# A DFT mixer and a 16-head attention on one core: the two middle rows of the sequence matrix prepared once, new durations in the planner, a second buffer for the spread maxima

## The chip, the core and the metric

The kernel runs on one core of one Trainium2 chip. A core has five engines that run side by side, each through its own list of instructions in order: TensorE (PE, matrix products, with its weight loads shown as PEld), VectorE (DVE), ScalarE (ACT), GpSimd (POOL) and SyncE (SP), which here issues every transfer. The metric is device time in microseconds of one launch. Before the change it was 798.91 us, the median of three runs (797.62 to 800.2).

## The reference

Two independent halves write the left and the right 448 columns of one output of 2048 rows.

```python
# A: Fourier mixing, real part
a = einsum("bsd,ed->bse", x, dft_hid_re);  b = einsum("bsd,ed->bse", x, dft_hid_im)
y = einsum("ts,bse->bte", dft_seq_re, a) - einsum("ts,bse->bte", dft_seq_im, b)
# B: attention, 16 heads of 28
q, k, v = split_heads(x @ wqkv)
o = softmax(q @ k.T * 28 ** -0.5) @ v
return concatenate([y, o @ wo], axis=-1)
```

`x` is 2048 x 448 in both, the sequence matrices `dft_seq_re` and `dft_seq_im` are 2048 x 2048, all in float32. Products are made in two parts, a rounded high part and the rest as a low part, so that the fast matrix format keeps enough digits.

## The kernel before

**The attention.** Part B projects `x` to queries, keys and values and keeps them in device memory. For each of 16 heads it computes scores in tiles of 128 keys by 512 queries (line 1155), takes the exponential from PSUM to a buffer called `kept` on ScalarE (line 1161), and multiplies with the values (line 1138). There are 16 buffers (pairs) called `kept`, and many steps borrow them. For the first tile of keys of each head, `first_tiles` takes the largest score per query and spreads it: VectorE turns the scores in blocks (line 1101) into a buffer `mb`, reduces them (line 1102), gathers (1108 to 1113), and for four chunks of queries turns the maxima back into `mb` (line 1122). From there they go to one row of `q` (line 1125, VectorE or GpSimd) and are added to the scores (line 1127, VectorE or GpSimd) ahead of the exponential (line 1129). There is one `mb`, so a second chunk can't be turned until line 1127 of the first has read it. The scores of the other key tiles need the row written by line 1125.

**The Fourier half.** The sequence matrices are symmetric about their middle, so the kernel works with 8 folded tiles of 128 inputs and 8 of 128 outputs. `hidden` makes the hidden transform of the folded `x`, for the real part and then for the imaginary part (line 900), and adds up `acc` for output row 1024 (line 921; from it comes the small product at line 1253). `sequence` then multiplies by the sequence matrix: for each of 8 output tiles and each half `g` (0 or 1) it loads four blocks of 256 KB: `w` (line 580), and the three others at line 638, two of them from a turned copy `wr` of the matrix. `w` is rounded on GpSimd (line 458) and its low part taken (line 591). `mirrored` compares the four blocks with each other: differences (lines 654, 672; "either" engine), single columns (lines 659, 662; "small"), and largest absolute values (line 645, VectorE), which decide at the end whether the matrices have the symmetry that the fast path takes for granted. If they had not, a slow general path would run. The blocks live in 8 buffers called `wraw`, and a buffer can take the next load only after line 645 has read it.

The first row and row 1024 have no partner, and enter by one more matmul for each output tile: three rows of the summed row `ext` against `peaks`, the hidden transform of the inputs 0 and 1024. In the kernel before, `mirrored` makes `ext` for each tile when `g` is 0, out of row 0 of the sum of line 672, by four VectorE instructions on 1 x 128 elements: line 677 rounds it, line 678 copies it, line 679 takes the low part, line 681 clears the row in the block. That is done 16 times.

**What sets the order.** Nothing is reordered by hand or by the chip. Each step is handed to a planner (`Schedule`) with a key (when it is wanted), the engines that may do it, a duration for each engine, and the buffers it takes. The planner plays all engines forward by these durations: an engine that is free takes the ready step with the smallest key, and the step is emitted there. So durations in the code change nothing about an instruction, but they decide which of VectorE and GpSimd gets a step, and in which order the five engines and the transfers run. On the chip each engine then waits, in that order, for what is not done.

The table of these durations is spread over the code: `either = {"POOL": 1.25, "DVE": 0.69}` and `small = {"POOL": 0.2, "DVE": 0.15}` for `mirrored`, 0.35 us for line 921, 0.8 us on VectorE for line 1127, 0.15 and 0.12 for `ext`.

Of the kernel before, what the change touches and what calls it, by code (L numbers as in the profile page):

```python
# [11 lines left out]
F32 = mybir.dt.float32  # L12
# [338 lines left out]
def tile_kernel(ctx, tc, xa, wre, wim, wd, xb, wqkv, wo, out):  # L351
# [33 lines left out]
    x_raw, x_hl = new("xraw", [P, NH, 4], F32), new("xhl", [P, 2, NH, 4], F32R)  # L385
    ext_s, peaks = new("ext", [P, P], F32R, 2), new("peak", [P, 2, E], F32R)
    w_hi, w_lo = new("whi", [P, 3, 4, P], F32R), new("wlo", [P, 3, 4, P], F32R)
# [5 lines left out]
    kept_s = new("kept", [P, 2, CH], F32, NKEPT)  # L393
    mb_s = new("mb", [P, CH], F32, 1, True)
    sm_s = new("sm", [P, 2, NT], F32, 2)
# [47 lines left out]
    def dve(key, emit, d=DVE_P, **kw):  # L443
        return sch.add({"DVE": d}, key, lambda e: emit(), **kw)
# [129 lines left out]
    class Piece:  # L574


        def __init__(self, src, key, kind="c", early=False, home=None, after=(), wide=False):
            self.hi, self.lo = whi.slot(), wlo.slot()
            raw = self.raw = home or wraw.slot()
            ld = self.ld = dma(key, lambda: nc.sync.dma_start(raw.t, src()), deps=after, acq=[raw])  # L580
            if kind == "c":
                a = sch.add({"POOL": 1.0, "ACT": ACT_S} if wide else {"POOL": 1.0}, key + 1, lambda g: eng_copy(g, self.hi.t, raw.t),
                            deps=[ld], acq=[self.hi], use=[raw])
            else:
                a = act(key + (0 if early else 1), lambda: nc.scalar.activation(self.hi.t, raw.t, AF.Copy), ACT_S, soon=SOON,  # L585
                        deps=[ld], acq=[self.hi], use=[raw])
            at = key + (0 if early else 1.5)
            both = ("DVE",) if early else ("POOL", "DVE") if wide else ("POOL",)
            e = {g: {"DVE": 0.8, "POOL": 1.25}[g] for g in both}
            n = 4 if kind == "c" else 3  # L590
            b = sch.add(e, at, lambda g: eng[g].tensor_tensor(  # L591
                self.lo.t[:, :n], raw.t[:, :n], f32(self.hi.t)[:, :n], op=ALU.subtract),
                deps=[a], acq=[self.lo], use=[raw, self.hi])
            self.ready, self.hi_ready, self.lo_ready = [b], a, [b]
            if kind == "w":
                self.ready.append(sch.add({g: {"DVE": 0.3, "POOL": 0.53}[g] for g in both}, at, lambda g: eng[g].tensor_tensor(
                    self.lo.t[:64, 3], raw.t[:64, 3], f32(self.hi.t)[:64, 3], op=ALU.subtract),
                    deps=[a, b], use=[raw, self.hi, self.lo]))
# [48 lines left out]

    either = {"POOL": 1.25, "DVE": 0.69}
    small = {"POOL": 0.2, "DVE": 0.15}

    def mirrored(part, tt, g, w, w2, w3, w4, left, right, key):
# [22 lines left out]
        if g == 0:  # L674
            ext = ext_s.slot()
            row = lambda: w2.raw.t[:1, 3, :]
            c = dve(key, lambda: nc.vector.tensor_copy(ext.t[:1], row()), 0.15, deps=[a, *ext_clear], acq=[ext], use=[w2.raw])
            c = dve(key, lambda: nc.vector.tensor_copy(ext.t[32:33], f32(ext.t)[:1]), 0.12, deps=[c], use=[ext])
            c = dve(key, lambda: nc.vector.tensor_tensor(ext.t[64:65], row(), f32(ext.t)[:1], op=ALU.subtract), 0.12,
                    deps=[c], use=[ext, w2.raw])  # L680
            a = dve(key, lambda: nc.vector.memset(row(), 0.0), 0.1, deps=[c], use=[w2.raw])
        else:
            ext, c = None, None
        largest(lambda: w2.raw.t, [a], part, key + 1, [w2.raw])
        return ext, c

    edge_done, edge_free = {}, {}
    far_done = []
# [146 lines left out]
    ext_clear += [pool(41.0, lambda: nc.gpsimd.memset(f32(peaks), 0.0), 0.57)]  # L835
    for i, t in enumerate(ext_s.tiles):
        ext_clear.append(pool(42.0 + i, lambda t=t: nc.gpsimd.memset(f32(t), 0.0), 0.3))
    ld = [dma(112.0 + 3 * k, lambda k=k: nc.sync.dma_start(x_raw[:, :, k], xa[NH:, :, k, 0].rearrange("t p -> p t")), 64, 2.0) for k in range(4)]
# [21 lines left out]
    class Pair:  # L860


        def __init__(self, i, part, key):
# [12 lines left out]
            c = sch.add({"DVE": 0.3, "POOL": 0.53}, key + 1.5, lambda g: eng[g].tensor_tensor(  # L876
                self.hi.t[64:, 3:], raw.t[64:, 3:], f32(self.hi.t)[64:, 3:], op=ALU.subtract), deps=[a], use=[raw, self.hi])
            self.ready = [b, c]

    def hidden(part, weights, ready, after):  # L880
# [25 lines left out]
        for i in range(NH):  # L906
# [10 lines left out]
                    deps=[t], use=[o, ut])  # L917
            a = act(key - 10, lambda ut=ut, uh=uh: nc.scalar.activation(uh, ut.t, AF.Copy), 0.3, soon=SOON, deps=[t, *after], use=[ut])
            b = sch.add({"POOL": 0.62, "DVE": 0.35}, key - 10, lambda e, ut=ut, uh=uh, ul=ul: eng[e].tensor_tensor(
                ul, ut.t, f32(uh), op=ALU.subtract), deps=[a], use=[ut])  # L920
            acc_done.append(dve(key - 5, lambda ut=ut, i=i: nc.vector.scalar_tensor_tensor(
                acc[:, part], ut.t, mid[:, part, i:i + 1], acc[:, part], op0=ALU.mult, op1=ALU.add), 0.35,
                deps=[t, got, acc_done[-1]], use=[ut]))
            if i == 0:
# [25 lines left out]
    def sequence(part, made, tiles=range(NH), late=False, free=()):  # L950
        src, wr = wim if part else wre, wr_d[part]
        u = u_of[part]
        for tt in tiles:
            o, pair = fill_s.slot(), kept_s.slot()
            for g in range(2):
# [13 lines left out]
                x, x_ready = mirrored(part, tt, g, w, w2, w3, w4, left, right, key - 8)  # L969
                if g == 0:  # L970
                    ext, ext_ready = x, x_ready
                jobs = []
                for k in range(4):
                    i = 4 * g + k
                    pair2 = [(w.hi, k, u[:, i, :], [w.hi_ready], w.hi, i), (w.lo, k, u[:, i, :E], w.ready, w.lo, i)]
                    if g and k == 3:
                        jobs.append((ext, None, peaks[:65, part], [ext_ready, *done_top[part]], ext, 0))
                        pair2.reverse()
                    jobs += pair2
                for n, (slot, k, b, ready, use, i) in enumerate(jobs):  # L980
                    first, final = g == 0 and n == 0, g == 1 and n == 8

                    def emit(e, o=o, slot=slot, k=k, b=b, first=first, final=final):
                        a = slot.t[:65] if k is None else slot.t[:, k, :]
                        nc.tensor.matmul(o.t[:, :2 * E if slot.pool is whi else E], a, b, start=first, stop=final)  # L985
                    deps = [last[0], *ready]
                    if tt == 0:
                        deps += made[i]
                    last[0] = pe(key + n * M225, emit, d=M448 if slot.pool is whi else M225, deps=deps, acq=[o] if first else [],
                                 use=[use, *([] if first else [o])])  # L990
                    if first:
# [3 lines left out]
                if part == 0:  # L995
                    if tt == 0 and g == 0:
                        turn_edges(1, last[0], key)
                    for n in range(2):
                        turn_rows(1, (tt * 2 + g) * 2 + n, last[0], key)
            key = key - 60  # L1000
            if part == 0:
# [4 lines left out]
            else:  # L1006
# [4 lines left out]
                b = dve(key, lambda o=o, q=q: nc.vector.tensor_tensor(q(), o.t[:, E:2 * E], q(), op=ALU.add), 0.35, deps=[b], use=[o, py])  # L1011
                w2 = {"DVE": 0.35, "POOL": 0.62}
                parts = {}
# [70 lines left out]
    def first_tiles(h):  # L1084
# [34 lines left out]
        for c in range(NC):  # L1119
# [6 lines left out]
                               deps=[t], use=[mb, q]))  # L1126
            sh = sch.add({"DVE": 0.8, "POOL": POOL_2}, key, lambda e, s=s, mb=mb: eng[e].tensor_tensor(s.t, s.t, mb.t, op=ALU.add),  # L1127
                         deps=[t, made[c]], use=[s.pair, mb], lat=LAT_S)
# [356 lines left out]
```

## Time and profile before

| what | value |
|---|---|
| median of three runs | 798.91 us (797.62 to 800.2) |
| the profiled execution, its time | 797.84 us |
| its span, first to last instruction | 796.2 us |
| mean granted TensorE clock | 0.973 |
| PE busy | 757.2 us (95%) |
| ACT busy | 610.7 us (77%) |
| DVE busy | 533.2 us (67%) |
| POOL busy | 336.5 us (42%) |
| DMA, share of 16 engines | 55.1% |

Busy time of PE counts matmuls whose ends are modelled, so a busy PE need not be at its peak. A granted clock under 1 means that the chip let TensorE run at less than full speed for part of the time. "Idle before, releaser" in a row of groups tells what an engine waited for just ahead of those instructions. The chain of waits starts at the last instruction and goes back, at each step, to what released it.

### The profile page before, as it was taken

What the parts mean: (1) busy time and instruction counts of PE and PEld (TensorE: products, weight loads), DVE (VectorE), ACT (ScalarE), POOL (GpSimd) and SP (SyncE); (2) the same over time, 40 slices, a digit from 0 to 9 for tenths busy, and PEclk for the clock granted to TensorE, in tenths of its full rate; (3) what the DMA queues carried; (4) which work ended last, traced back from release to release, by engine and by line L of the source; (5) the groups of instructions that cost most, each with busy time, mean ns of one, the idle gap of its engine ahead of it and who ended that gap; (6) DMA issues with size and microseconds to landing.
All of it is one profiled execution on the core that took longest, in us unless ns stands there. A gap on an engine that the chain in (4) does not pass through costs nothing.

```text
span 796.2 us, 13074 instructions
## 1 busy us (share of the span) xinstructions
PE 757.2 (95%) x4150; PEld 428.5 (54%) x4150; DVE 533.2 (67%) x1039; ACT 610.7 (77%) x1232; POOL 336.5 (42%) x410
## 2 busy tenths in 40 slices
PE   9999999999999998988899999998988799999997
PEld 7898655555555553454345554444444344334496
DVE  5547814465466869898887967796967878244371
ACT  6403798989898988887688979896876768898932
POOL 7301301414032535566573716274767754022510
PEclk9999999999999999999799999999998999999999
DMA  8957836472428456726477666646556462305254
GB/s 307 289 207 219 250 115 182 150 224 85 130 63 231 145 160 179 222 71 198 131 222 189 195 172 194 182 129 198 176 171 210 154 191 74 88 19 171 80 172 145
DMA packets 113541, 133.15 MB, mean 167 GB/s; under 512 B 50314, under 2 KB 63145, under 8 KB 113465
## 3 DMA queue, kind: packets, MB, share of 16 engines
q1 hardware_dynamic: 113464, 132.24, 55.1%
q8 instruction: 35, 0.57, 0.3%
q14 instruction: 42, 0.34, 0.1%
HBM read 101.15 MB, written 49.19 MB: 189 GB/s over the span
## 4 chain that ended last, share of the span: by engine, by line
PE 68%; DVE 18%; DMA 6%; ACT 4%; issue 2%; SPq 0%; POOL 0%; DVEq 0%; ACTq 0%
PE bank L1155 22%; PE bank L1138 21%; PE bank L726 12%; PE bank L1317 4%; DMA wraw<-wr 4%; ACT kept L1161 3%; PE bank L985 3%; DVE far L645 2%; PE bank L762 2%; PE bank L900 2%; PE bank L1096 1%; DVE mb L1101 1%; DVE qm L1102 1%; DVE kept L1127 1%; DVE q L1125 1%
## 5 line engine op out<-in xcount | busy, mean ns | idle before, releaser
L1161 ACT ACTIVATE kept<-bank 128x512 f32<-128x512 f32 x960 | 485.8, 646 | 83.7 <-PE bank L1155 82.6
L1155 PE MATMUL bank<-q,k 98*128 98x512 f32 x960 | 343.4, 430 | 17.7 <-ACT kept L1161 11.7
L1155 PEld LDWEIGHTS bank<-q,k 98*128 98x128 f32 x960 | 174.5, 190 | 191.1 <-issue 99.2
L1138 PE MATMUL bank<-kept,v 128*32 128x512 f32 x2048 | 251.4, 615 | 0.0
L1138 PEld LDWEIGHTS bank<-kept,v 128*32 128x32 f32 x2048 | 55.8, 111 | 121.1 <-issue 116.3
L1127 POOL TENSOR_TENSOR kept<-kept,mb 128x512 f32<-128x512 f32 x39 | 55.5, 1423 | 70.0 <-DVE mb L1122 52.2
L1100 ACT ACTIVATE kept<-bank 128x512 f32<-128x512 f32 x64 | 38.4, 653 | 35.2 <-PE bank L1096 22.6
L1101 DVE STREAM_TRANSPOSE mb<-bank 128x512 f32<-128x512 f32 x64 | 45.5, 711 | 26.9 <-PE bank L1096 23.6
L1198 POOL TENSOR_TENSOR kept<-kept 128x512 f32<-128x512 f32 x16 | 20.6, 1288 | 96.3 <-DVE kept L1193 78.6
L645 DVE TENSOR_REDUCE far<-wraw 128x1 f32<-128x508 f32 (+1 forms) x90 | 57.5, 657 | 1.1 <-POOL wraw L672 0.7
L726 PE MATMUL bank<-big,whi 128*128 128x512 f32 x154 | 56.6, 396 | 0.0
L1122 DVE STREAM_TRANSPOSE mb<-am 128x512 f32<-128x512 f32 x64 | 45.1, 705 | 11.8 <-POOL kept L1127 10.3
L591 POOL TENSOR_TENSOR wlo<-wraw,whi 128x512 fp32r<-128x512 f32 (+1 forms) x34 | 45.0, 1324 | 18.8 <-ACT whi L585 16.8
L985 PE MATMUL bank<-big,whi 128*128 128x452 f32 x128 | 49.8, 390 | 3.1 <-POOL whi L458 3.1
L1129 ACT ACTIVATE kept<-kept 128x512 f32<-128x512 f32 x64 | 43.0, 704 | 10.1 <-POOL kept L1127 5.6
L654 POOL TENSOR_TENSOR wraw<-wraw,wraw 128x508 f32<-128x508 f32 x35 | 38.6, 1104 | 23.6 <-DMA wraw<-wr 19.6
L1102 DVE TENSOR_REDUCE qm<-mb 128x16 f32<-128x512 f32 x64 | 43.4, 678 | 1.2
L1125 POOL CAST q<-mb 1x512 fp32r<-1x512 f32 x20 | 13.5, 673 | 71.5 <-DVE mb L1122 55.3
L726 PE MATMUL bank<-wd,big 128*128 128x448 f32 x176 | 36.8, 364 | 0.0
L985 PE MATMUL bank<-big,wlo 128*128 128x226 f32 x128 | 35.8, 279 | 0.9 <-POOL wlo L591 0.9
L1189 DVE STREAM_TRANSPOSE kept<-kept 128x512 f32<-128x512 f32 x16 | 11.2, 702 | 35.5 <-ACT kept L1187 35.5
L726 PE MATMUL bank<-big,wlo 128*128 128x512 f32 x88 | 34.8, 396 | 0.0
(167 smaller groups left out, 966.3 us busy)
## 6 DMA issues: line engine op xcount, KB each, us to landing
wraw<-wr SPq DMA_DIRECT2D x60, 256.0 KB
qkd<-kept SPq DMA_DIRECT2D x40, 256.0 KB
wraw<-xa SPq DMA_DIRECT2D x32, 256.0 KB
wraw<-wre SPq DMA_DIRECT2D x32, 256.0 KB
wr<-wre SPq DMA_DIRECT2D x31, 256.0 KB
wr<-wim SPq DMA_DIRECT2D x31, 256.0 KB
k<-qkd SPq DMA_DIRECT2D x64, 112.0 KB
q<-qkd SPq DMA_DIRECT2D x64, 112.0 KB
```

What stands on the lines that cost most here:

```text
L591: b = sch.add(e, at, lambda g: eng[g].tensor_tensor(self.lo.t[:, :n], raw.t[:, :n], f32(self.hi.t)[:, :n], op=ALU.subtract), deps=[a], acq ...
L645: far_done.append(dve(key, lambda: nc.vector.tensor_reduce(far[:, part, n:n + 1], t(), axis=AX.XY, op=ALU.max, apply_absolute_value=True), ...
L726: nc.tensor.matmul(o.t[:, :cols], w(), x(), start=(i == 0), stop=(i == n - 1))
L985: nc.tensor.matmul(o.t[:, :2 * E if slot.pool is whi else E], a, b, start=first, stop=final)
L1101: t = dve(key, lambda o=o, tm=tm: nc.vector.transpose(tm.t, o.t), 0.73, deps=[m], acq=[tm], use=[o], lock=[o], own=RAW_S)
L1102: rs.append(dve(key, lambda tm=tm, c=c: nc.vector.tensor_reduce(qm.t[:, 0, c * NT:(c + 1) * NT], tm.t.rearrange("p (j r) -> p j r", r=32), ...
L1122: t = dve(key, lambda mb=mb, c=c: nc.vector.transpose(mb.t, f32(am.t)[:, c * NT:(c + 1) * NT].unsqueeze(2).to_broadcast([P, NT, 32])), 0.7 ...
L1127: sh = sch.add({"DVE": 0.8, "POOL": POOL_2}, key, lambda e, s=s, mb=mb: eng[e].tensor_tensor(s.t, s.t, mb.t, op=ALU.add), deps=[t, made[c] ...
L1129: shown.append(act(key, lambda s=s: nc.scalar.activation(s.t, s.t, AF.Exp, scale=SCALE), ACT_S, deps=[sh], use=[s.pair]))
L1138: nc.tensor.matmul(o.t[c * VW:(c + 1) * VW, :], VT[h].t[:, kt // 4, kt % 4, :], tiles[c].t, start=(kt == 0), stop=(kt == NT - 1))
L1155: m = pe(key, lambda e, o=o, q=q, kt=kt: nc.tensor.matmul(o.t, KT[h][kt // 4].t[:KM, kt % 4 * P:(kt % 4 + 1) * P], q.t[:KM, :], start=True ...
L1161: es[h, kt].append(act(key - 20, lambda o=o, p=p: nc.scalar.activation(p.t, o.t, AF.Exp, scale=SCALE), deps=[m], use=[o, p.pair]))
```

## The change

Four edits, of which the third and the fourth are spread over several places.

1. `ext` is no longer made for each output tile. A new function `middle(part, ...)` loads rows 0 and 1024 of the matrix, 8 x 128 elements each, onto one partition (two transfers of 4 KB into two `kept` buffers), combines them, and writes the three rows for all eight tiles at once, 1 x 1024 elements, into a part of `big` that is free by then. It is called for the real part behind the fifth tile of `hidden(0)` and for the imaginary part at the seventh output tile of the real part. The four steps may run on GpSimd or VectorE; one GpSimd memset goes ahead of them. The matmul takes its 128 columns out of that strip. Only the clearing of the row in the block (line 681) stays in `mirrored`. The two `ext` buffers and their two memsets go.
2. `mb` gets a second buffer.
3. Durations that the planner reckons with are set to other values, most of them higher on VectorE, some lower on GpSimd.
4. The matmul's step in `sequence` no longer takes an `ext` buffer.

```diff
-    ext_s, peaks = new("ext", [P, P], F32R, 2), new("peak", [P, 2, E], F32R)
+    peaks = new("peak", [P, 2, E], F32R)
-    mb_s = new("mb", [P, CH], F32, 1, True)
+    mb_s = new("mb", [P, CH], F32, 2, True)
...
-                a = sch.add({"POOL": 1.0, "ACT": ACT_S} if wide else {"POOL": 1.0}, key + 1, lambda g: eng_copy(g, self.hi.t, raw.t),
+                a = sch.add({"POOL": 0.75, "ACT": ACT_S} if wide else {"POOL": 0.75}, key + 1, lambda g: eng_copy(g, self.hi.t, raw.t),
-            e = {g: {"DVE": 0.8, "POOL": 1.25}[g] for g in both}
+            e = {g: {"DVE": 0.85, "POOL": 1.35}[g] for g in both}
...
-    either = {"POOL": 1.25, "DVE": 0.69}
-    small = {"POOL": 0.2, "DVE": 0.15}
+    either = {"POOL": 1.2, "DVE": 0.83}
+    small = {"POOL": 0.35, "DVE": 0.4}
...
         if g == 0:
-            ext = ext_s.slot()
-            row = lambda: w2.raw.t[:1, 3, :]
-            c = dve(key, lambda: nc.vector.tensor_copy(ext.t[:1], row()), 0.15, deps=[a, *ext_clear], acq=[ext], use=[w2.raw])
-            c = dve(key, lambda: nc.vector.tensor_copy(ext.t[32:33], f32(ext.t)[:1]), 0.12, deps=[c], use=[ext])
-            c = dve(key, lambda: nc.vector.tensor_tensor(ext.t[64:65], row(), f32(ext.t)[:1], op=ALU.subtract), 0.12,
-                    deps=[c], use=[ext, w2.raw])
-            a = dve(key, lambda: nc.vector.memset(row(), 0.0), 0.1, deps=[c], use=[w2.raw])
-        else:
-            ext, c = None, None
+            a = dve(key, lambda: nc.vector.memset(w2.raw.t[:1, 3, :], 0.0), 0.17, deps=[a], use=[w2.raw])
...
+    def middle(part, key, dep):
+        src, pairs = (wre, wim)[part], [kept_s.slot() for _ in range(2)]
+        h = NH * P
+        op = ALU.add if part else ALU.subtract
+        ext = big[:, 2 * NT * E + part * h:2 * NT * E + (part + 1) * h]
+        row = lambda i: pairs[i].t.rearrange("p a b -> p (a b)")[:1, :h]
+        z = pool(key, lambda: nc.gpsimd.memset(f32(ext)[:65], 0.0), 1.1, deps=[dep])
+        ld = [dma(key + 0.1 * i, lambda i=i: nc.sync.dma_start(
+            row(i).rearrange("p (a b) -> p a b", a=NH), src[:NH, :1, NH * i, :].rearrange("t p s -> p t s")), 8, 2.0,
+            deps=[dep], acq=[pairs[i]]) for i in range(2)]
+        both = {"POOL": 1.5, "DVE": 1.3}
+        a = sch.add(both, key + 1, lambda g: eng[g].tensor_tensor(row(1), row(1), row(0), op=op), deps=ld, use=pairs)
+        b = sch.add(both, key + 1, lambda g: eng[g].tensor_copy(ext[:1], row(1)), deps=[a, z], use=[pairs[1]])
+        c = sch.add(both, key + 1, lambda g: eng[g].tensor_copy(ext[32:33], f32(ext)[:1]), deps=[b])
+        d = sch.add(both, key + 1, lambda g: eng[g].tensor_tensor(ext[64:65], row(1), f32(ext)[:1], op=ALU.subtract),
+                    deps=[b], use=[pairs[1]])
+        middles[part] = ext, [c, d]
...
-    for i, t in enumerate(ext_s.tiles):
-        ext_clear.append(pool(42.0 + i, lambda t=t: nc.gpsimd.memset(f32(t), 0.0), 0.3))
...
-            a = pool(key + 1, lambda: nc.gpsimd.tensor_copy(self.hi.t, raw.t), 1.0, deps=[b], acq=[self.hi], use=[raw])
-            b = sch.add(either, key + 1.5, lambda g: eng[g].tensor_tensor(
+            a = pool(key + 1, lambda: nc.gpsimd.tensor_copy(self.hi.t, raw.t), 0.7, deps=[b], acq=[self.hi], use=[raw])
+            b = sch.add({"POOL": 1.08, "DVE": 0.58}, key + 1.5, lambda g: eng[g].tensor_tensor(
...
-                acc[:, part], ut.t, mid[:, part, i:i + 1], acc[:, part], op0=ALU.mult, op1=ALU.add), 0.35,
+                acc[:, part], ut.t, mid[:, part, i:i + 1], acc[:, part], op0=ALU.mult, op1=ALU.add), 0.7,
...
+            if part == 0 and i == 4:
+                middle(0, key, a)
...
-                        jobs.append((ext, None, peaks[:65, part], [ext_ready, *done_top[part]], ext, 0))
+                        jobs.append((None, None, peaks[:65, part], [*ext_ready, *done_top[part]], None, 0))
...
-                        a = slot.t[:65] if k is None else slot.t[:, k, :]
+                        a = ext[:65, tt * P:(tt + 1) * P] if k is None else slot.t[:, k, :]
...
+            if part == 0 and tt == NH - 2:
+                middle(1, key, last[0])
...
-                w2 = {"DVE": 0.35, "POOL": 0.62}
+                w2 = {"DVE": 0.64, "POOL": 0.7}
...
-            sh = sch.add({"DVE": 0.8, "POOL": POOL_2}, key, lambda e, s=s, mb=mb: eng[e].tensor_tensor(s.t, s.t, mb.t, op=ALU.add),
+            sh = sch.add({"DVE": 0.92, "POOL": POOL_2}, key, lambda e, s=s, mb=mb: eng[e].tensor_tensor(s.t, s.t, mb.t, op=ALU.add),
```

Left out of the diff: line 918 is planned at 0.45 us for 0.3, line 919 at 0.77 (GpSimd) or 0.64 (VectorE) for 0.62 or 0.35, and line 876 at 0.5 on VectorE for 0.3.

More of the change, by code (lines that the diff above doesn't have):

```diff
@@ L674, in mirrored @@
         if g == 0:
-            ext = ext_s.slot()
-            row = lambda: w2.raw.t[:1, 3, :]
-            c = dve(key, lambda: nc.vector.tensor_copy(ext.t[:1], row()), 0.15, deps=[a, *ext_clear], acq=[ext], use=[w2.raw])
-            c = dve(key, lambda: nc.vector.tensor_copy(ext.t[32:33], f32(ext.t)[:1]), 0.12, deps=[c], use=[ext])
-            c = dve(key, lambda: nc.vector.tensor_tensor(ext.t[64:65], row(), f32(ext.t)[:1], op=ALU.subtract), 0.12,
-                    deps=[c], use=[ext, w2.raw])
-            a = dve(key, lambda: nc.vector.memset(row(), 0.0), 0.1, deps=[c], use=[w2.raw])
-        else:
-            ext, c = None, None
-        largest(lambda: w2.raw.t, [a], part, key + 1, [w2.raw])
-        return ext, c
+            a = dve(key, lambda: nc.vector.memset(w2.raw.t[:1, 3, :], 0.0), 0.17, deps=[a], use=[w2.raw])
+        largest(lambda: w2.raw.t, [a], part, key + 1, [w2.raw])
+    def middle(part, key, dep):
[15 more added lines that the diff above has]
+        middles[part] = ext, [c, d]
+    middles = {}
     edge_done, edge_free = {}, {}
@@ L872, in __init__ @@
                 raw.t[:, :, 0], x_raw[:, back], raw.t[:, :, 0], op=op), deps=[a, *x_col], use=[raw])
-            a = pool(key + 1, lambda: nc.gpsimd.tensor_copy(self.hi.t, raw.t), 1.0, deps=[b], acq=[self.hi], use=[raw])
-            b = sch.add(either, key + 1.5, lambda g: eng[g].tensor_tensor(
+            a = pool(key + 1, lambda: nc.gpsimd.tensor_copy(self.hi.t, raw.t), 0.7, deps=[b], acq=[self.hi], use=[raw])
+            b = sch.add({"POOL": 1.08, "DVE": 0.58}, key + 1.5, lambda g: eng[g].tensor_tensor(
                 self.lo.t[:, :3], raw.t[:, :3], f32(self.hi.t)[:, :3], op=ALU.subtract), deps=[a], acq=[self.lo], use=[raw, self.hi])
-            c = sch.add({"DVE": 0.3, "POOL": 0.53}, key + 1.5, lambda g: eng[g].tensor_tensor(
+            c = sch.add({"DVE": 0.5, "POOL": 0.53}, key + 1.5, lambda g: eng[g].tensor_tensor(
                 self.hi.t[64:, 3:], raw.t[64:, 3:], f32(self.hi.t)[64:, 3:], op=ALU.subtract), deps=[a], use=[raw, self.hi])
@@ L917, in hidden @@
                     deps=[t], use=[o, ut])
-            a = act(key - 10, lambda ut=ut, uh=uh: nc.scalar.activation(uh, ut.t, AF.Copy), 0.3, soon=SOON, deps=[t, *after], use=[ut])
-            b = sch.add({"POOL": 0.62, "DVE": 0.35}, key - 10, lambda e, ut=ut, uh=uh, ul=ul: eng[e].tensor_tensor(
+            a = act(key - 10, lambda ut=ut, uh=uh: nc.scalar.activation(uh, ut.t, AF.Copy), 0.45, soon=SOON, deps=[t, *after], use=[ut])
+            b = sch.add({"POOL": 0.77, "DVE": 0.64}, key - 10, lambda e, ut=ut, uh=uh, ul=ul: eng[e].tensor_tensor(
                 ul, ut.t, f32(uh), op=ALU.subtract), deps=[a], use=[ut])
             acc_done.append(dve(key - 5, lambda ut=ut, i=i: nc.vector.scalar_tensor_tensor(
-                acc[:, part], ut.t, mid[:, part, i:i + 1], acc[:, part], op0=ALU.mult, op1=ALU.add), 0.35,
+                acc[:, part], ut.t, mid[:, part, i:i + 1], acc[:, part], op0=ALU.mult, op1=ALU.add), 0.7,
                 deps=[t, got, acc_done[-1]], use=[ut]))
@@ L968, in sequence @@
                         0.65, deps=[w.ld], use=[w.raw]))
-                x, x_ready = mirrored(part, tt, g, w, w2, w3, w4, left, right, key - 8)
-                if g == 0:
-                    ext, ext_ready = x, x_ready
+                mirrored(part, tt, g, w, w2, w3, w4, left, right, key - 8)
+                ext, ext_ready = middles[part]
                 jobs = []
@@ L981, in sequence, with emit @@
                     first, final = g == 0 and n == 0, g == 1 and n == 8
-                    def emit(e, o=o, slot=slot, k=k, b=b, first=first, final=final):
-                        a = slot.t[:65] if k is None else slot.t[:, k, :]
-                        nc.tensor.matmul(o.t[:, :2 * E if slot.pool is whi else E], a, b, start=first, stop=final)
+                    def emit(e, o=o, slot=slot, k=k, b=b, first=first, final=final, tt=tt, ext=ext):
+                        a = ext[:65, tt * P:(tt + 1) * P] if k is None else slot.t[:, k, :]
+                        nc.tensor.matmul(o.t[:, :2 * E if slot and slot.pool is whi else E], a, b, start=first, stop=final)
                     deps = [last[0], *ready]
@@ L988, in sequence @@
                         deps += made[i]
-                    last[0] = pe(key + n * M225, emit, d=M448 if slot.pool is whi else M225, deps=deps, acq=[o] if first else [],
-                                 use=[use, *([] if first else [o])])
+                    last[0] = pe(key + n * M225, emit, d=M448 if slot and slot.pool is whi else M225, deps=deps, acq=[o] if first else [],
+                                 use=[*([use] if use else []), *([] if first else [o])])
                     if first:
```

## The prediction

> **What bounds the kernel now.** I read the kernel in stretches first, since its page says that PE is 95% busy and an average hides where it is not. The columns of the view by stretches are the length, then busy time (and instructions) of PE, PEld, DVE, ACT and POOL, the granted TensorE clock, the DMA share and GB/s.
>
> ```profile
> 6.00:280.00 274.00, 273.99 (x1501) 174.04 (x1504) 158.04 (x319) 209.25 (x420) 79.81 (x98) 1.00 0.61 186
> 280.00:380.00 100.00, 90.62 (x535) 45.89 (x527) 87.08 (x167) 82.01 (x171) 56.54 (x73) 0.99 0.57 167
> 380.00:560.00 180.00, 171.45 (x961) 88.02 (x965) 146.70 (x270) 146.54 (x292) 94.42 (x111) 0.95 0.61 180
> 560.00:665.00 105.00, 91.71 (x480) 44.75 (x476) 83.76 (x158) 74.53 (x148) 69.03 (x83) 0.90 0.56 172
> ```
>
> Up to 280 us PE never stops and VectorE is busy for 158 of 274 us. From 280 to 665 us, where `mirrored` runs, VectorE is busy 317.5 of 385 us and PE stands still for 9.4 + 8.5 + 13.3 = 31.2 us. The clock falls with it: 0.01 x 100 + 0.05 x 180 + 0.10 x 105 = 20.5 us of full speed are missing. So 51.7 us are lost in this stretch, 27.9 of them before 560 (17.9 idle, 10.0 of clock) and 23.8 behind it (13.3 and 10.5). These are what the change can reach.
>
> Then I read whom PE waited for: total, times, longest.
>
> ```profile
> PE bank L1155 <- ACT kept L1161: 11.7, 11, 3.2
> PE bank L1253 <- DVE kept L1251: 6.0, 1, 6.0
> PE bank L985 <- DVE ext L679: 4.4, 2, 2.8
> ```
>
> ScalarE is only the last in a row there: followed back, the chain of waits goes through VectorE. This is its piece at the first output tile (start, length, what):
>
> ```profile
> 297.08 0.71 DVE mb L1101
> 297.79 0.87 DVE ext L677
> ...
> 300.03 1.11 DVE ext L679
> ...
> 301.19 0.37 PE bank L985
> ```
>
> PE stands until the third `ext` instruction ends at 301.14. Behind 560 us the chain looks otherwise:
>
> ```profile
> 590.37 8.48 DMA wraw<-wim
> ...
> 617.31 1.20 DVE ext L678
> 619.05 1.72 DVE far L645 x3
> 620.80 7.70 DMA wraw<-wr
> ...
> 642.64 8.52 DMA wraw<-wr
> ```
>
> Here loads that take 7.7 to 8.5 us are in the chain. A load waits for line 645 to free its buffer (the second piece starts right behind one), so VectorE's lateness comes first, but the landing itself isn't VectorE's.
>
> Last I read the groups in 280 to 665 us, for what each VectorE instruction takes (busy total, mean ns of one) beside what the planner believes.
>
> ```profile
> L654 DVE TENSOR_TENSOR wraw<-wraw,wraw 128x508 f32<-128x508 f32 x24 | 20.8, 866 | 5.8 <-DMA wraw<-wr 4.3 <-DMA wraw<-wre 0.8 <-DMA wraw<-wim 0.5
> L645 DVE TENSOR_REDUCE far<-wraw 128x1 f32<-128x512 f32 x30 | 19.9, 665 | 0.8 <-POOL wraw L672 0.7
> L458 POOL CAST whi<-wraw 128x512 fp32r<-128x512 f32 x27 | 19.3, 715 | 22.8 <-DMA wraw<-wim 11.4 <-PE bank L985 10.6 <-DMA wraw<-wre 0.8
> L1125 DVE CAST q<-mb 1x512 fp32r<-1x512 f32 x19 | 17.3, 910 | 0.6
> L1127 DVE TENSOR_TENSOR kept<-kept,mb 128x512 f32<-128x512 f32 x17 | 17.0, 1002 | 0.2
> ...
> L659 DVE TENSOR_TENSOR off<-edge,wraw 128x4 f32<-128x4 f32 x30 | 10.4, 364 | 10.6 <-DMA wraw<-wim 7.7 <-DMA wraw<-wre 1.7 <-DMA wraw<-wr 1.2
> L672 DVE TENSOR_TENSOR wraw<-wraw,wraw 128x512 f32<-128x512 f32 x11 | 8.3, 758 | 1.1 <-POOL wraw L654 1.1
> L678 DVE CAST ext<-ext 1x128 fp32r<-1x128 f32 x15 | 8.3, 550 | 0.4
> L677 DVE CAST ext<-wraw 1x128 fp32r<-1x128 f32 x15 | 8.1, 540 | 0.9 <-PE bank L985 0.8
> L1016 POOL TENSOR_TENSOR kept<-py 128x225 f32<-128x225 f32 x11 | 7.6, 706 | 3.6 <-DVE py L1011 1.8 <-ACT kept L1161 1.0 <-DMA wraw<-wim 0.8
> L921 DVE SCALAR_TENSOR_TENSOR acc<-ut,mid,acc 128x226 f32<-128x226 f32 x10 | 7.4, 744 | 0.3
> L679 DVE TENSOR_TENSOR ext<-wraw,ext 1x128 fp32r<-1x128 f32 x15 | 7.4, 491 | 0.2
> ...
> L662 DVE COPY edge<-wraw 128x4 f32<-128x4 f32 x20 | 7.2, 361 | 4.8 <-DMA wraw<-wr 4.0 <-POOL off L659 0.8
> ```
>
> The work that VectorE does and the planner does not reckon with is count times (mean less planned): `ext` 15 x (0.540 + 0.550 + 0.491 - 0.15 - 0.12 - 0.12) = 17.9 us; lines 659 and 662, 30 x 0.214 + 20 x 0.211 = 10.6; line 654, 24 x 0.176 = 4.2; line 1125, 19 x 0.21 = 4.0; line 921, 10 x 0.394 = 3.9; line 1127, 17 x 0.202 = 3.4; line 672, 0.7. Together 44.7 us. Line 645, at 0.665 for 0.65, is right. My reading is that **this 44.7 us is why PE arrives before its operands**: the order is drawn for a VectorE that is 44.7 us faster.
>
> **The change part by part.** *Rows prepared once.* It takes 15 x 1.581 = 23.7 us off VectorE in the stretch and all 17.9 us of the unreckoned time. It adds, for each part, two casts and two subtractions on 1 x 1024, a length that the trace does not show. From below, they cost what 1 x 128 costs (0.55 and 0.49), 4.2 us for both parts; from above, twice 1 x 512 (line 1125, 0.910) and twice 128 x 512 (line 1127, 1.002), 2 x (2 x 1.82 + 2 x 2.00) = 15.3 us. I take the upper, as length is what these rows share. The planner reckons with 2 x 4 x 1.3 = 10.4, so 4.9 us are unreckoned anew (at the lower end -6.2). If GpSimd does them, nothing is: it is free for 385 - 220 = 165 us there. Its two memsets of 1024 columns cost at most 2 x 0.715 each (line 458), 2.9 us, in that free time; the two small ones that go were made early, before 280 us, where GpSimd is free for 194 of 274 us.
>
> The four transfers of 4 KB and the eight steps must be done before the first `peaks` matmul of their part. Times of first and last start end these rows:
>
> ```profile
> L900 PE MATMUL bank<-wd,whi x64: 362/372/379, 229.0 to 372.4; 128*128 128x452 f32 x64
> ```
>
> ```profile
> L985 PE MATMUL bank<-peak,ext x16: 265/268/392, 301.2 to 749.3; 65*128 65x226 f32 x16
> ```
>
> The eight tiles of `hidden(0)` start at 229.0 and the first `peaks` matmul comes at 301.2; behind the fifth of eight tiles some 30 us of that are left. `middle` needs a load of 8.5 us (the longest in the chain above) and 2.0 + 1.82 + 2.0 in a row, 14.3 us. So I cost it at nothing, hidden under three tiles of `hidden` and the first half tile; with the cover gone it would be 14.3 us, once for each part, less for the second with a whole output tile between. It holds two of sixteen `kept` buffers for about as long, 0 to 2 us if an exponential wants one; I take 0. SP issues four transfers more than before, among hundreds.
>
> *Durations.* By the same rows the new values leave unreckoned: line 654, 24 x 0.036 = 0.9; 921, 0.4; 1127, 1.4; 1125, 4.0; 659 and 662 nothing (0.4 planned), 672 nothing. With `ext` gone, 38.1 of the 44.7 us go and 4.9 come, so 33.2, or 74%.
>
> *Second `mb`.* What it can save is a wait of VectorE:
>
> ```profile
> DVE mb L1122 <- POOL kept L1127: 10.3, 9, 1.2
> ```
>
> Nine waits of about 1 us in the whole execution; in the 274 us before 280, where VectorE is free for 116 us and PE never stops, they cost nothing. I take 0, at most a wait or two of 1.2 us.
>
> *The sum.* I let the loss before 560 us follow the unreckoned time: 0.74 x 27.9 = 20.7 us. This goes from at least 4.4 us, PE's direct wait for `ext`, to all of 27.9. Of the 23.8 us behind 560 I take only the 1.2 us of line 678 that precedes the load at 620.80; at most it follows too, 17.6 us. The profiled execution is 797.84 us, 1.07 below the median. 797.84 - 20.7 - 1.2 = 775.9, so **776 us**, and for this case alone 764 to 791.
>
> **The rivals.** *The waits pass on.* The same `ext` instruction has very different times (least, median, most):
>
> ```profile
> L678 DVE CAST ext<-ext x16: 217/220/1323, 299.3 to 732.6; 1x128 fp32r<-1x128 f32 x16
> ```
>
> Its own work is 0.22 us; the mean of 0.550 holds waits for something else. If the VectorE instruction behind it inherits such a wait, only 0.217 / 0.550 = 39% of the 23.7 us are saved, 9.3, and 14.4 of the 38.1 us come back under another line: 38.1 - 14.4 - 4.9 = 18.8, 42% of 44.7. That gives 797.84 - 0.42 x 27.9 - 0.5 = **785.6 us**. For it: the reduce of line 645 has no second source and shows no such spread in its mean (0.665 for 0.65). Against: the wait may end with the GpSimd instruction that caused it, before the next one starts.
> [...]
>
> *All of it follows.* The loads behind 560 are late because line 645 frees their buffers late, and an honest order cures both: 797.84 - 0.74 x 51.7 = **759.6 us**. For it: the piece at 617 to 620.80; against: 8.5 us from issue to landing stays.
>
> *Late loads become the bound: slower.* With longer VectorE times the planner frees `wraw` later, puts loads later into SP's single list, and each goes behind other transfers. Behind 560 us three such loads stand in the chain for 23.8 us lost, 7.9 each. If the denser order makes four more of them before 560, it costs 31.7 us; less the 21.9 gained this is 797.84 + 9.8 = **807.6 us**. It decides from three more late loads on (21.9 / 7.9 = 2.8). For it: nothing in the diff shortens a load. Against: before 560 us PE's waits end with VectorE or ScalarE.
>
> *No gain from it.* The order is drawn anew from 280 us on, and the stalls only move: the 4.4 us wait for `ext` goes and a wait like that of line 1253 or 1155 (longest 3.2) takes its place, **797 us**.
>
> **How the numbers follow.** A measurement tells about 0.3%, 2.4 us, from no change. Chances: forecast 0.42, waits pass on 0.19, all follows 0.18, no gain 0.08, late loads 0.13. The first three hold 0.79, of which I leave 0.01 to no change: 0.78 for faster. Of the 0.08 without gain, 0.01 falls on the slow side: 0.08 + 0.01 - 0.01 = 0.08 for the same, 0.13 + 0.01 = 0.14 for slower. The range takes in 759.6 with a little below it and reaches towards the late loads: 756 to 803.
>
> **What would show it.** Right: no row of `ext` on VectorE but the clearing, PE idle time from 280 to 560 us near 5 us for 17.9, clock near 0.99 there, VectorE's share down, line 654 and 1127 more often on GpSimd. The second rival shows as the means of lines 654, 659 and 1127 growing while VectorE's busy time falls by some 9 us only. The slower one shows as more chain pieces "DMA wraw" of 8 us. Wrong altogether would be a PE wait at the first `peaks` matmul for `middle`, or idle time before 560 us that stays although VectorE's unreckoned time is gone.

## The result, and the profile after

The changed kernel takes **773.05 us** (median of four, 771.07 to 773.51) against 798.26 us beside it: a ratio of 0.9678, 95% interval 0.965 to 0.9706. The profiled execution is 773.51 us, 24.3 less than the one before.

The view by stretches of the changed kernel, with the columns of the first fence of the prediction:

```profile
6.00:280.00 274.00, 273.71 (x1496) 172.28 (x1499) 151.98 (x305) 209.61 (x420) 78.04 (x101) 1.00 0.60 184
280.00:380.00 100.00, 94.56 (x550) 47.93 (x543) 84.69 (x152) 84.51 (x175) 67.50 (x82) 1.00 0.57 165
380.00:560.00 180.00, 176.46 (x992) 89.58 (x994) 144.07 (x244) 152.87 (x307) 107.43 (x123) 0.96 0.59 172
560.00:665.00 105.00, 98.83 (x562) 49.67 (x558) 91.20 (x160) 87.04 (x174) 77.10 (x95) 0.97 0.67 200
```

The gain is where it was sought. PE stands for 5.4 + 3.5 + 6.2 = 15.1 us from 280 to 665 us (31.2 before), and 0.04 x 180 + 0.03 x 105 = 10.3 us of clock are missing (20.5 before). The loss went from 51.7 to 25.5 us. But its places are others than forecast: before 560 us it fell by 11.7 us (27.9 to 16.2), behind 560 by 14.5 us (23.8 to 9.3). These are stretches of equal time, not of equal work: PE's first score matmul of head 12 comes at 566.5 us here and at 579.7 us before.

Whom PE waited for, in total:

```profile
PE bank L994 <- POOL whi L458: 5.2, 3, 2.4
PE bank L1166 <- ACT kept L1172: 4.1, 9, 1.1
PE bank L1166 <- ACT kept L1111: 2.4, 2, 1.4
```

The waits for `ext` and for `acc`'s product (6.0 us) are gone or small, and what led before, the wait for an exponential (now line 1172), fell from 11.7 to 4.1 us. In front stands now a wait for GpSimd's rounding of a block.

The groups of the changed kernel in 280 to 665 us (line 1138 is the former 1127, 1136 the former 1125; lines 689 and 692 are the subtractions of `middle`):

```profile
L654 DVE TENSOR_TENSOR wraw<-wraw,wraw 128x508 f32<-128x508 f32 x27 | 27.1, 1006 | 7.7 <-DMA wraw<-wr 5.1 <-DMA wraw<-wim 2.4
...
L1138 DVE TENSOR_TENSOR kept<-kept,mb 128x512 f32<-128x512 f32 x23 | 24.7, 1096 | 0.2
...
L1136 DVE CAST q<-mb 1x512 fp32r<-1x512 f32 x18 | 18.2, 1026 | 0.4
...
L662 DVE COPY edge<-wraw 128x4 f32<-128x4 f32 x14 | 7.9, 571 | 0.5 <-POOL off L659 0.3 <-DMA wraw<-wim 0.2
...
L689 POOL TENSOR_TENSOR kept<-kept,kept 1x1024 f32<-1x1024 f32 x2 | 5.1, 2550 | 4.1 <-DMA kept<-wre 4.1
L692 POOL TENSOR_TENSOR big<-kept,big 1x1024 fp32r<-1x1024 f32 x2 | 5.1, 2544 | 0.2
```

The three `ext` rows are gone. The first four lines shown all got slower on VectorE (1.006 for 0.866, 1.096 for 1.002, 1.026 for 0.910, 0.571 for 0.361 us), and the planner gave VectorE more of lines 654 and 1138, not less. GpSimd does the middle rows' subtractions, 2.55 us each, and VectorE their four casts, 4.6 us in all.

### The profile page after: what moved, and what is told of

The parts are those of the page before. It is cut to its first block, busy times and chain, and to the rows that moved or that the text cites. A ratio compares the mean times of both kernels' runs of the same rounds, so it can differ in the third digit from the quotient of the medians.

```text
span 771.8 us, 13016 instructions
## 1 busy us (share of the span) xinstructions
PE 748.9 (97%) x4150; PEld 425.8 (55%) x4150; DVE 521.2 (68%) x962; ACT 609.4 (79%) x1231; POOL 362.2 (47%) x448
## 4 chain that ended last, share of the span: by engine, by line
PE 72%; DVE 9%; DMA 6%; POOL 4%; ACT 4%; issue 3%; SPq 1%; POOLq 0%; ACTq 0%; DVEq 0%
PE bank L1166 24%; PE bank L1149 23%; PE bank L736 12%; PE bank L1328 5%; PE bank L994 4%; ACT kept L1172 3%; PE bank L772 2%; PE bank L908 2%; DMA wraw<-wim 2%; PE bank L1107 1%; DMA wr<-wim 1%; DMA wraw<-wr 1%; DVE kept L1138 1%; DVE mb L1133 1%; DVE mb L1112 1%
## 5 line engine op out<-in xcount | busy, mean ns | idle before, releaser
L1149 PE MATMUL bank<-kept,v 128*32 128x512 f32 x2048 | 247.8, 608 | 0.0
L1136 POOL CAST q<-mb 1x512 fp32r<-1x512 f32 x39 | 32.2, 842 | 79.4 <-DVE mb L1133 60.7
L1209 POOL TENSOR_TENSOR kept<-kept 128x512 f32<-128x512 f32 x16 | 20.7, 1291 | 80.4 <-DVE kept L1204 58.5
L994 PE MATMUL bank<-big,whi 128*128 128x452 f32 x128 | 48.2, 376 | 5.2 <-POOL whi L458 5.2
L1140 ACT ACTIVATE kept<-kept 128x512 f32<-128x512 f32 x64 | 41.2, 720 | 4.4 <-DVE kept L1138 3.7
L1133 DVE STREAM_TRANSPOSE mb<-am 128x512 f32<-128x512 f32 x64 | 43.3, 697 | 1.5 <-POOL q L1136 0.5
L1138 DVE TENSOR_TENSOR kept<-kept,mb 128x512 f32<-128x512 f32 x40 | 38.8, 986 | 0.2
L458 POOL CAST whi<-wraw 128x512 fp32r<-128x512 f32 x30 | 20.0, 665 | 37.1 <-DMA wraw<-wre 13.9
L1200 DVE STREAM_TRANSPOSE kept<-kept 128x512 f32<-128x512 f32 x16 | 11.2, 700 | 37.8 <-ACT kept L1198 37.8
L753 DVE TENSOR_TENSOR kept<-bank,kept 128x512 fp32r<-128x512 f32 x20 | 13.3, 687 | 34.3 <-ACT kept L752 34.2
```

What stands on the lines that cost most here:

```text
L994: nc.tensor.matmul(o.t[:, :2 * E if slot and slot.pool is whi else E], a, b, start=first, stop=final)
L1133: t = dve(key, lambda mb=mb, c=c: nc.vector.transpose(mb.t, f32(am.t)[:, c * NT:(c + 1) * NT].unsqueeze(2).to_broadcast([P, NT, 32])), 0.7 ...
L1138: sh = sch.add({"DVE": 0.92, "POOL": POOL_2}, key, lambda e, s=s, mb=mb: eng[e].tensor_tensor(s.t, s.t, mb.t, op=ALU.add), deps=[t, made[c ...
L1140: shown.append(act(key, lambda s=s: nc.scalar.activation(s.t, s.t, AF.Exp, scale=SCALE), ACT_S, deps=[sh], use=[s.pair]))
L1149: nc.tensor.matmul(o.t[c * VW:(c + 1) * VW, :], VT[h].t[:, kt // 4, kt % 4, :], tiles[c].t, start=(kt == 0), stop=(kt == NT - 1))
```

## The experiments

Each run stands beside runs of the kernel before; times are medians, with the ratio and its 95% interval.

### One part alone: rows, durations, second mb

Rows 0 and 1024 once, the rest as before: the changed kernel with the durations of the third edit set back (only the clearing of the row stays at 0.17 us), and

```diff
-    mb_s = new("mb", [P, CH], F32, 2, True)
+    mb_s = new("mb", [P, CH], F32, 1, True)
```

> The kernel before with the new function for rows 0 and 1024 alone: all durations as before, one mb. Theory 1 (the loss follows the VectorE time that the planner does not reckon with): 17.9 of 44.7 us go and at most 4.9 come, 29% of 27.9 us and 1.2 us at one load, about 9 us faster, 789 us. Theory 2 (waits pass on to the next VectorE instruction): 3 us faster, 795 us. Theory 3 (the order drawn anew is what counts, whatever the reason): anything between 780 and 810, with no relation to VectorE's time.

Measured: **778.36 us**, 0.9751 (0.9715 to 0.9787), 18.7 us faster: twice what theory 1 gave, and below the 780 us of theory 3 as well.

The durations alone, the whole third edit put into the kernel before:

```diff
-    either = {"POOL": 1.25, "DVE": 0.69}
-    small = {"POOL": 0.2, "DVE": 0.15}
+    either = {"POOL": 1.2, "DVE": 0.83}
+    small = {"POOL": 0.35, "DVE": 0.4}
...
```

> The kernel before with the new durations alone: ext is still made for each tile, planned at its old 0.15 and 0.12 us, one mb. Theory 1: 20.2 of 44.7 us of unreckoned time go, 45% of 27.9 us, about 12.6 us faster, 786 us. Theory 2: the same, 786 us. Theory 3: anything between 780 and 810.

Measured: **778.27 us**, 0.9755 (0.9716 to 0.9793), 18.8 us faster, again more than any of the three theories gave.

The second `mb` alone, in the kernel before:

```diff
-    mb_s = new("mb", [P, CH], F32, 1, True)
+    mb_s = new("mb", [P, CH], F32, 2, True)
```

> The kernel before with a second mb alone. Theory 1 and 2: no VectorE time changes, 798 us, within 3 us of it. Theory 3 (an order drawn anew counts by itself): the planner draws another order here too, so that the time can move by 5 us or more either way.

Measured: **770.9 us**, 0.9658 (0.961 to 0.9705), 26 us faster: as much as the whole change, from the edit that I had costed at nothing. Theories 1 and 2, at 798 us, are out for it. Each of the three parts takes most of the same loss, and 19 + 19 + 26 us is more than the 51.7 us there were. That raised the question whether the order of before is just a poor draw.

### The draw

Two numbers of the planner, each in a kernel of its own, moved by a hair in the kernel before:

```diff
-PE_TURN = 0.33
+PE_TURN = 0.34
```

```diff
-    def pe(key, emit, n=1, d=MS, lat=0.25, **kw):
+    def pe(key, emit, n=1, d=MS, lat=0.255, **kw):
```

> The kernel before with one number of the planner moved by a hair, the planner's price for PE turning to the value products, 0.33 to 0.34 us: nothing is reckoned better or worse, only the order comes out another way from some point on. Theory A (the order of before is a poor draw, and nearly any new draw is better): 775 to 790 us. Theory B (it takes less VectorE time, better reckoning or a second mb to gain): 792 to 804 us, scattered about 797 us.

> The kernel before with another such hair: the planner's latency of a matmul's result 0.25 to 0.255 us. Theory A: 775 to 790 us. Theory B: 792 to 804 us. Both nudges together tell how wide times scatter by the draw alone.

Measured: **792.19 us**, 0.9931 (0.9907 to 0.9955), and **796.16 us**, 0.9985 (0.9962 to 1.0009). The order moves in hundreds of places and the time by 0.5 to 4.4 us. Two draws are few, but 19 to 26 us from any draw at all (theory A) is out, and a single draw's worth of some 5 us has to be granted to every run that changes the order.

### VectorE's time, in one and the same order

In the kernel before, three planned steps issue nothing:

```diff
-            c = dve(key, lambda: nc.vector.tensor_copy(ext.t[:1], row()), 0.15, ...
-            c = dve(key, lambda: nc.vector.tensor_copy(ext.t[32:33], f32(ext.t)[:1]), 0.12, ...
-            c = dve(key, lambda: nc.vector.tensor_tensor(ext.t[64:65], row(), ...), 0.12, ...
+            c = dve(key, lambda: None, 0.15, ...
+            c = dve(key, lambda: None, 0.12, ...
+            c = dve(key, lambda: None, 0.12, ...
```

> The kernel before with its order kept to the instruction: the planner still plans the three ext instructions of each tile, but they are not issued, so ext stays zero and the share of inputs 0 and 1024 is left out of the left half of the output. Theory 1: all 17.9 us of unreckoned time go and nothing comes, 40% of 27.9 us and 1.2 us, about 12 us faster, 786 us. Theory 2: 5 us faster, 793 us, with the means of lines 654, 1125 and 1127 on VectorE growing by the 14 us that the ext lines lost. Theory 3: the order is the same, so that only the two direct waits of 4.4 us go, 794 us, with no growth of these means.

Measured: **781.92 us**, 0.9813 (0.9783 to 0.9842), 15.1 us faster, with no instruction moved. So VectorE's lateness is a cause by itself, and it costs nearer 15 than the 12 us of theory 1; the 5 us of theory 2 and the 4.4 us of theory 3 are out. Of the 15.1 us, 4.4 are PE's two direct waits for `ext`, which are gone from the trace; the rest came by other ways. The view by stretches over the whole execution, for the kernel before and for this run, shows how much VectorE was relieved (third busy column):

```profile
0.00:800.00 800.00, 757.16 (x4150) 428.46 (x4150) 533.15 (x1039) 610.66 (x1232) 336.53 (x410) 0.97 0.55 166
```

```profile
0.00:800.00 800.00, 750.27 (x4150) 427.11 (x4150) 515.63 (x991) 610.86 (x1232) 336.49 (x410) 0.98 0.55 166
```

The three lines had 24.5 us (23.8 in the rows of the prediction, the rest in the sixteenth tile); VectorE's busy time fell by 17.5. The other 7.0 us, 29%, came back in other lines. At their shortest (171, 217 and 282 ns) these 48 instructions would take 10.7 us, so by my estimate some 13.8 of the 24.5 us were waits, and about half of the waits came back. The groups of this run over the whole execution, whose counts are those of the prediction's rows:

```profile
L659 DVE TENSOR_TENSOR off<-edge,wraw 128x4 f32<-128x4 f32 x30 | 11.9, 413 | 10.6 <-DMA wraw<-wim 7.9 <-DMA wraw<-wre 1.6 <-DMA wraw<-wr 1.0
...
L662 DVE COPY edge<-wraw 128x4 f32<-128x4 f32 x20 | 9.7, 483 | 5.5 <-DMA wraw<-wr 5.1 <-POOL kept L1127 0.3
L672 DVE TENSOR_TENSOR wraw<-wraw,wraw 128x512 f32<-128x512 f32 x11 | 9.4, 857 | 1.1 <-POOL wraw L654 1.1
```

0.413 for 0.364 us, 0.483 for 0.361, 0.857 for 0.758: 1.5 + 2.4 + 1.1 = 5.0 of the 7.0 us. So waits do pass on, about half of them, but not to the lines that theory 2 had named: in the same views the means of lines 654, 1125 and 1127 are 0.874, 0.704 and 0.954 us for 0.858, 0.725 and 0.943 before.

Where the time went shows in the stretches of this run:

```profile
280.00:380.00 100.00, 94.02 (x541) 47.19 (x533) 87.50 (x168) 84.95 (x177) 61.77 (x81) 0.98 0.59 174
380.00:560.00 180.00, 175.58 (x1026) 90.66 (x1025) 145.69 (x259) 154.65 (x309) 100.28 (x116) 0.99 0.63 189
560.00:665.00 105.00, 93.29 (x500) 46.34 (x496) 75.85 (x139) 79.95 (x160) 64.25 (x77) 0.92 0.52 160
```

Ahead of 560 us the loss fell from 27.9 to 14.2 us (10.4 idle, 3.8 of clock), behind it only from 23.8 to 20.1 (11.7 and 8.4). VectorE's lateness costs time mostly where the prediction had put it.

### What the second mb does

In the kernel before, the planner goes on seeing one `mb`, and the chunks use two in turn (`Turn` gives the tile `mb_2[c % 2]`; line 1101's buffer likewise):

```diff
     mb_s = new("mb", [P, CH], F32, 1, True)
+    mb_2 = [mb_s.tiles[0], sb.tile([P, CH], F32, tag="mb1", name="mb1")]
...
-            q, s, mb = Q[h][c], R[h][0][c], mb_s.slot()
+            q, s, own = Q[h][c], R[h][0][c], mb_s.slot()
+            mb = Turn(own, c)
```

> The kernel before, planned as with one mb, so in the order of before, but the chunks take two buffers in turn on the chip. Theory C (the second buffer gains by itself, through waits of VectorE for line 1127 that it removes): 780 us or less, as with the second mb that the planner knew. Theory D (it gains only through the other order that the planner draws with it): 795 to 798 us, as only 1.6 of the 11.8 us that line 1122 waited lie behind 280 us.

Measured: **795.3 us**, 0.9988 (0.9967 to 1.0009). In the old order a second buffer gains nothing that can be told from no change: the wait for line 1127, 10.3 us in the kernel before, is gone from this run's trace and was worth nothing, as forecast. The 26 us come through what the planner does once it knows of two. VectorE's order around head 12 shows it, from the kernel before:

```profile
565.50 0.71 DVE L1122 STREAM_TRANSPOSE mb<-am 128x512 f32<-128x512 f32 x1
566.81 1.11 DVE L1125 CAST q<-mb 1x512 fp32r<-1x512 f32 x1
571.42 0.69 DVE L1122 STREAM_TRANSPOSE mb<-am 128x512 f32<-128x512 f32 x1
572.61 0.67 DVE L1127 TENSOR_TENSOR kept<-kept,mb 128x512 f32<-128x512 f32 x1
575.71 0.69 DVE L1122 STREAM_TRANSPOSE mb<-am 128x512 f32<-128x512 f32 x1
576.90 0.79 DVE L1127 TENSOR_TENSOR kept<-kept,mb 128x512 f32<-128x512 f32 x1
578.80 0.69 DVE L1122 STREAM_TRANSPOSE mb<-am 128x512 f32<-128x512 f32 x1
```

and with the second `mb` alone:

```profile
548.36 1.30 DVE L1122 STREAM_TRANSPOSE mb<-am 128x512 f32<-128x512 f32 x2
...
551.57 0.71 DVE L1122 STREAM_TRANSPOSE mb<-am 128x512 f32<-128x512 f32 x1
...
554.70 0.70 DVE L1122 STREAM_TRANSPOSE mb<-am 128x512 f32<-128x512 f32 x1
```

With one buffer the planner must put line 1127 of a chunk, and its result's latency, between two turns, and fills the gaps on VectorE with `mirrored`: the four turns of a head take 14.0 us. With two they take 7.0 us. And PE's first score matmul of the head (line 1155, sixty to a head) comes at 579.7 us before, 0.9 us behind the start of the last turn, and at 562.7 us with two, 8.0 us behind it. Over heads 6 to 14 this distance is -4.4 to 5.4 us before and 8.0 to 11.2 us with two. I call it margin. It is a measure of the room that VectorE has, not the room itself: the first matmul needs only the row of the first chunk, and the fourth is the first to need the row of the last turn. From the end of line 1125 for the last chunk to that fourth matmul it is 0.1 to 5.2 us before and 6.5 to 10.6 us with two; by so much can this row come later before PE stands for it. PE's direct wait for the row was one of 2.3 us before and is gone with two, so most of the 26 us comes by ways that this reading does not show.

### Does the margin take up the lateness?

The same three steps issue nothing, in the kernel with the second `mb` alone:

```diff
-    mb_s = new("mb", [P, CH], F32, 1, True)
+    mb_s = new("mb", [P, CH], F32, 2, True)
...
+            c = dve(key, lambda: None, 0.15, ...
...
```

> The run with the second mb alone, its order kept to the instruction, but the three ext instructions of each tile are planned and not issued, so ext stays zero and the share of inputs 0 and 1024 is left out of the left half of the output. Theory M (the second mb gives margin: PE's first score matmul of a head comes 8 to 11 us behind the start of the last turn of line 1122 for 1 to 5 us in the kernel before, and this margin takes up VectorE's lateness): the same 24 us of VectorE time now gain 5 us or less, 766 to 771 us. Theory N (lateness costs the same wherever the order is from): 15 us as in the order of before, about 756 us.

Measured: **765.91 us**, 0.9618 (0.9579 to 0.9658), 5.0 us under the run with the second `mb` alone by the medians, and 3.2 us by the two ratios, whose intervals overlap: a small gain, or none. The 15 us of theory N are out. The same instructions left out, in an unchanged order both times, gain 15.1 us in the order with little margin and some 5 in the one with 8 to 11 us. That is what theory M forecast; that the margin, and nothing else in the other order, makes the difference is not shown by this run, and the next one asks for it.

Margin by another way, in the kernel before:

```diff
-        key0 = begins[h] - 26
+        key0 = begins[h] - 34
```

> The kernel before, one mb, ext for each tile, old durations; only the keys of a head's first tiles are put 8 us earlier (34 us ahead of the head for 26), so that the planner makes the margin in another way than by a second mb. Theory M: most of the gain of the second mb, 773 to 785 us, with the first score matmul of a head 8 us or more behind the start of the last turn of line 1122. If the second mb gained by something else than this margin: 790 to 800 us.

Measured: **786.46 us**, 0.9883 (0.9842 to 0.9924), 9.8 us faster: between the two forecasts. The margin was made (8.2 to 12.0 us for eight of heads 6 to 14, 5.7 for one), but the turns stay spread over 9 to 15 us, and new waits came. PE's waits in this run:

```profile
PE bank L1155 <- DVE mb L1101: 3.5, 4, 1.1
PE bank L1096 <- DMA q<-qkd: 3.3, 2, 3.0
PE bank L985 <- DVE ext L679: 2.8, 1, 2.8
```

So margin bought by starting earlier gains some 10 us, of which some 5 may be the draw; theory M's "most of the gain" did not come. What makes up the other 16 us of the second `mb`, the turns standing together or the new waits here, these runs do not separate.

### Do the parts add up, and what is left?

The changed kernel with one `mb`:

```diff
-    mb_s = new("mb", [P, CH], F32, 2, True)
+    mb_s = new("mb", [P, CH], F32, 1, True)
```

> The changed kernel with one mb: rows once and new durations. If each edit takes its own share (19 us each alone), 760 us can't be, as 51.7 us are all there is; if they share the same loss, about 775 us, within 5 us of the changed kernel. If the second mb carries the change, 785 us or more.

Measured: **772.01 us**, 0.9702 (0.9658 to 0.9745). Rows and durations alone reach what all three reach; beside them the second `mb` gains nothing. I read this as two cures of one loss, less lateness and more margin: in this run the margin of heads 6 to 14 is only -2.2 to 4.4 us. With the rows alone it is -0.4 to 6.9 us, with the durations alone 0.7 to 4.9, so neither of these gains by margin.

The changed kernel with the planner's landing time of loads longer, and, as another kernel, with durations measured once more:

```diff
-(3.0 if T_IN - 6 < now < 42 else 0.0)
+(3.0 if T_IN - 6 < now < 42 else 2.5 if size > 200 and now > 200 else 0.0)
```

```diff
-    either = {"POOL": 1.2, "DVE": 0.83}
+    either = {"POOL": 1.2, "DVE": 1.0}
-            row.append(sch.add({"DVE": 0.7, "POOL": 0.7}, ...
+            row.append(sch.add({"DVE": 1.0, "POOL": 0.85}, ...
...
```

> The changed kernel, with the planner told that loads of over 200 KB land 2.5 us later from 200 us on. What is left of PE's waits ends with lines 458 and 591 on blocks that arrived late (6.5 us of 17.8 in all). If late landings are what is left: 4 to 10 us faster than the changed kernel, 763 to 769 us. If they only follow from VectorE's lateness: within 3 us of 773 us.

> The changed kernel with the durations measured in it put into the planner once more: VectorE 1.0 us for line 654's kind, 1.05 for the addition of the spread maxima, 1.0 (GpSimd 0.85) for the row of q, 0.5 for the gathering copies, 0.8 for acc, GpSimd 2.5 for the middle rows' subtractions. Some 19 us of VectorE time that the changed kernel's planner does not reckon with go. Theory 1 without a limit (the loss follows the unreckoned time): 10 us or more faster, 763 us or less. Theory M: with the margin there, little is left to gain, 768 to 775 us.

Measured: **769.41 us**, 0.9662 (0.9625 to 0.9698), and **768.25 us**, 0.9642 (0.9595 to 0.9689). Both medians lie under the changed kernel's, but their intervals and its own overlap; neither is shown to beat it, nor is the second `mb` alone (0.961 to 0.9705). The longer landing time comes out between its two forecasts and decides nothing. Telling the planner the truth a second time gains a few us by the medians, within the 768 to 775 us of theory M.

## Why the prediction was right, and where its steps were wrong

**The total** came out at 773.05 us for 776 forecast. The step that carried it, that VectorE's time which the planner does not reckon with makes PE's operands late, is shown for the part that could be isolated: 15.1 us from leaving out three instructions per tile in an unchanged order. But the sum reached the total with terms of the wrong size, whose errors cancel: that it came so near is in good part luck.

**"Second mb: I take 0."** This step failed. Its reading of the wait was right (0.9988 in the old order), but it priced the buffer by the wait that it removes and not by the order that it allows. Alone it is worth 26 us. It did not spoil the total only because the other two edits had taken the same loss already (772.01 us without it).

**The proportion, 0.74 x 27.9.** A rule of the form "the loss follows the unreckoned time" does not hold across orders. In the changed kernel the same lines leave 27 x 0.176 + 23 x 0.176 + 18 x 0.326 + 14 x 0.171 us, with line 921's 1.2 some 18 us for 44.7, 59% gone, and 51% of the loss went with it. That looks like proportion. But with the second `mb` alone all of `ext` and all wrong durations are still there, and the time fell as far (770.9 us). The rule left out what the order itself does; the margin with which it places PE's need behind VectorE's work is the part of this that the runs show.

**"Of the 23.8 us behind 560 I take only 1.2."** Wrong: 14.5 us went there. Ahead of 560, 11.7 us went and not 20.7, and the two errors cancel to within 5 us. The rival "all of it follows" has this amount, but its reason, loads that are late because VectorE frees their buffers late, is not borne out. With VectorE relieved in an unchanged order, 20.1 of the 23.8 us stayed, and loads of 7.1 to 8.7 us stood in the chain there as before. With the second `mb` alone, and VectorE no less busy (536.5 for 533.2 us in all), 12.1 us were left, and with the rows alone 21.6:

```profile
560.00:665.00 105.00, 98.15 (x545) 48.62 (x537) 88.80 (x167) 84.12 (x167) 66.62 (x77) 0.95 0.61 182
```

So behind 560 us it was mainly the planner's other order that gained, and not VectorE's shorter work. What in that order did it stays open.

**Unreckoned time left over.** Forecast 6.7 us and 4.9 for the middle rows; measured 18 and none. The means of lines 654, 1125 and 1127 on VectorE grew by 0.09 to 0.14 us, and the forecast that GpSimd would get more of lines 654 and 1127 was wrong: VectorE has 27 and 23 of them for 24 and 17. Other signs failed with it: PE's idle time from 280 to 560 us is 9.0 us and not near 5, and VectorE's busy time from 280 to 665 us did not fall (320.0 for 317.5 us). The growing means are the sign that the rival of waits that pass on had named; but its time, 785.6 us, did not come.

**Waits pass on.** The rival let 61% of the saved time come back, as if every wait passed on; in one order it was 29%, about half of the waits. In the run of the same order without `ext`, lines 659, 662 and 672 inherit 5.0 us; lines 654 and 1127, which read two operands as 659 and 672 do, kept their means within 0.02 us (654 on the blocks of `wraw`). Why a wait goes to the one line and not to the other is not shown.

**`middle` costs nothing.** Right in effect, but by luck. No PE wait stands at the `peaks` matmul; yet of the 30 us of cover little was left. The start of the last steps of the two parts and the first `peaks` matmul:

```profile
L692 POOL TENSOR_TENSOR big<-kept,big x2: 2384/2544/2705, 301.8 to 517.9; 1x1024 fp32r<-1x1024 f32 x2
```

```profile
L994 PE MATMUL bank<-peak,big x16: 265/269/275, 306.9 to 725.3; 65*128 65x226 f32 x16
```

The strip of the real part is ready at 304.2 us (the last subtraction starts at 301.8 and takes 2.38) and wanted at 306.9. The zeroing of the strip ran at 276.9 us, but its loads were issued only at 290.9; GpSimd waited 4.1 us for them (row of line 689 above), and its subtractions took 2.55 us for 1.5 planned. My cover was counted from when `middle` could start, not from where the planner put its loads.

**The slower rival**, late loads as the bound, did not come: PE's waits for line 458 are 5.2 us in all.

## What to carry to other kernels

In an order fixed beforehand, a buffer count or a duration acts twice: by the wait on the chip, and by the places that the planner gives to everything else. Price an edit of this kind not by the wait in the trace alone, but also by the distance between the end of the producer's work and the consumer's place in its list; here that told more than the wait, though not all. And when several edits aim at one loss, ask first how much of it there is: here each alone took 19 to 26 us of it, and all together 25.

## What the runs showed of the hardware

In the kernel before, PE's granted clock fell to half behind one wait of PE of some 1.6 us, and not behind another. Two stretches of 20 us, in order of time:

```profile
340.00:360.00 20.00, 17.95 (x107) 9.76 (x110) 19.26 (x36) 17.63 (x38) 13.35 (x19) 1.00 0.18 57
520.00:540.00 20.00, 18.42 (x107) 8.45 (x102) 19.53 (x33) 15.80 (x32) 15.59 (x14) 0.91 0.38 123
```

In the first PE has one wait of 1.57 us, and one of 0.48; in the second it has one of 1.58 us alone. The first loses none of its clock, the second 9%, which is 1.8 us of full speed. The wait of 1.57 us ends at 357.75 us, and the granted clock stays 1.00 up to 375 us; the one of 1.58 us ends at 533.92, and from 535.1 to 538.4 us the granted clock is 0.50. Why two waits of the same length end differently, no run here shows.

GpSimd took 2.55 us to subtract 1 x 1024 elements on one partition (line 689), and 1.29 us to multiply 128 x 512 (line 1198 before). One subtraction of the kernel before comes at two heights: line 452 took 1.15 us for 64 x 448 elements and 1.18 us for 128 x 448. In these rows its time went with the elements in a row, not with the rows.
